# Two heads per load for values as well as keys, in one ring of three 64-KB slots, in a one-core decode block

## The chip, the cores and the metric

The kernel runs on one core of a Trainium2 chip. The metric is the device time in microseconds of one execution; the time before is the median of three runs. A profile of one further execution gives the span, what each engine did and what the DMA engines moved.

## The reference

One token (x, 640 wide) goes through an attention block over a cache of 16384 positions and 32 heads, and then a gated feed-forward block. Both are conditioned by a vector c (adaptive layer norm).

```python
mod = (silu(c) @ w_mod)                      # 640 -> 6 x 640
sa, ca, ga, sb, cb, gb = mod's six parts
h = layernorm(x) * (1 + ca) + sa
q = (h @ wq) as 32 heads of 128
scores = q . k_cache * 128 ** -0.5           # k_cache: 32 heads x 16384 x 128, bf16
p = softmax(scores)
o = p . v_cache                              # v_cache: 32 heads x 16384 x 128, bf16
x = x + ga * (o as one row of 4096 @ wo)
h = layernorm(x) * (1 + cb) + sb
x = x + gb * ((silu(h @ w_gate) * (h @ w_up)) @ w_down)
```

Keys and values are 134 MB each; every byte is read once and used for one multiplication.

## The kernel before, in words

**The order of work.** The kernel lists operations, each with an engine, a position (a number) and the operations it depends on. Each engine's list is sorted by position, so an engine runs its list in order and a wait holds up whatever is behind it. All large loads are issued from the sync engine's list (L71) into one queue, whose transfers run one after the other. `BU(u)` and `EU(u)` are the planned begin and end of unit u; they only order the lists.

**Keys, on VectorE.** A unit is two heads (15 units; the last two heads are units of one). A load of two heads puts 64 KB in each of 128 partitions: 64 partitions per head, 256 positions in each. In place, VectorE multiplies the keys by the query, which is laid out over the partitions (`qbc`, L577, in two pieces), folds the 128 products of a position to 64, 32 and 16 by adding halves (L600; L595 for the first fold of unit 0), and reduces 16 to one score (`S_sb`, L602). Then comes the maximum per partition (L604). The keys lie in `kbig`, two slots of 64 KB per partition: the keys of unit u+2 are loaded once L602 of unit u is done.

**Softmax.** TensorE turns the maxima to a row (L464), VectorE takes the top of each head (L466), TensorE spreads it (L474), ScalarE takes the exponentials (`P_k`, L492). The scores lie 64 partitions to a head, while the values lie 128 partitions to a head, so four products with `place` (L504) move the exponentials to that layout (`P_sb`, evacuated in L508).

**Values, on TensorE.** The values of one head are one load of 32 KB per partition into `vbig`, two slots of 32 KB. 32 products per head (L529) have four positions of `P_sb` as weights and 512 values as the moving side; ScalarE evacuates (L540), and per four heads L547 picks the right parts and turns them into columns (`OT_ps`). L554 divides by the softmax sum (L515 to L518), and L559 to L565 lay eight heads (four in the last group) out for the product with wo (L670). The last head's values come in three pieces and are multiplied position by position (L631). The last four heads' rows of wo come in a layout of their own.

**Before and after.** w_mod (one load of 37.5 KB per partition) and wq come ahead of the keys; w_mod's space is the second key slot, wq's the value slots. The first keys come in two halves. At the end wo goes into the first key slot, the feed-forward weights into the second (L733 gate and up, L751 down, whose weights come in pieces).

Of the kernel before, what the change touches and what calls it, by code (L numbers as in the profile page):

```python
# [141 lines left out]
def build(nc, A_x, A_k, A_v, A_wq, A_wo, B_wg, B_wu, B_wd, c_in, w_mod, out):  # L142
# [10 lines left out]
    GQ = 4  # L153
    PVB = 5
    NU = H // 2 - 1
    T2 = 2 * TT
    UNITS = [(2 * u, 2) for u in range(NU)] + [(H - 2, 1), (H - 1, 1)]

    GROUPS = [(0, 8), (8, 8), (16, 8), (24, 4)]
    HD = 28  # L160
    assert H % GQ == 0 and all(128 % n == 0 for _, n in GROUPS) and GROUPS[-1][0] + GROUPS[-1][1] == HD < H
# [4 lines left out]
    def BU(u):  # L166
        return 20.0 + PERIOD * UNITS[u][0]

    def EU(u):
        return BU(u) + 18.6 * UNITS[u][1]  # L170

    es = ExitStack()
    with es:
# [11 lines left out]
        KS = T2 * 128  # L185
        kbig = sb("kbig", [128, 2 * KS], BF16)
        vbig = sb("vbig", [128, 2 * TT * 128], BF16)
        vring = vbig[:].rearrange("p (s t d) -> p s t d", s=2, t=TT)
        assert max(WM_E, FFN_E, H * D) <= KS and WQ_E <= 2 * TT * 128
        wm_v = kbig[:, KS:KS + WM_E].rearrange("p (k n) -> p k n", k=KC)  # L190
        wq_v = vbig[:, 0:WQ_E].rearrange("p (k n) -> p k n", k=KC)
        wo_v = kbig[:, 0:H * D].rearrange("p (k n) -> p k n", k=H)
        wg_v = kbig[:, KS:KS + KC * F].rearrange("p (k n) -> p k n", k=KC)
        wu_v = kbig[:, KS + KC * F:KS + 2 * KC * F].rearrange("p (k n) -> p k n", k=KC)
        wd_v = kbig[:, KS + 2 * KC * F:KS + 2 * KC * F + FCH * D].rearrange("p (k n) -> p k n", k=FCH)
        acc_sb = sb("acc_sb", [128, 512], F32)
        sel = sb("sel", [128, 4, 4], F32)
        qbc = sb("qbc", [128, len(UNITS), 128], BF16)
        S_sb = sb("S_sb", [128, T2], F32)
        P_k = sb("P_k", [128, T2], BF16)  # L200
        P_sb = sb("P_sb", [128, 2, TT], BF16)
        ident_f = sb("ident_f", [128, 128], F32)
        place = sb("place", [128, 2, 2, 128], BF16)
        ramp = S_sb[:, 0:128]
        gm2 = sb("gm2", [1, 2], F32)
        ones_f = sb("ones_f", [128, 128], F32)
        ones_bf = sb("ones_bf", [128, 128], BF16)
# [3 lines left out]
        Z = sb("Z", [128, len(GROUPS), 128], BF16)  # L211
        A_sb = sb("A_sb", [128, HD], BF16)
        On = sb("On", [128, H - HD], BF16)
        x_row = sb("x_row", [KC, 128], BF16)
        o_row = sb("o_row", [KC, 128], BF16)
        x_res = sb("x_res", [128, KC], F32)
        c_one = acc_sb[0:1].bitcast(BF16)[:, 0:D]
        x_one = qbc[0:1].rearrange("p u d -> p (u d)")[:, 0:D]
        pm = sb("pm", [128, len(UNITS)], F32)
        nb = sb("nb", [128, len(UNITS)], F32)  # L220
        rs = sb("rs", [128, H], F32)
        lnl = sb("lnl", [128, H], F32)
# [38 lines left out]
        R_ps = f_ps[:, 0:2 * TT]  # L261
# [8 lines left out]
        o_onesf = op(DVE, 0.0, lambda e: e.memset(ones_f[:], 1.0), name="ones_f")  # L270
        o_ones = op(DVE, 0.01, lambda e: e.memset(ones_bf[:], 1.0), name="ones")


# [6 lines left out]
        o_pc = op(PE, 1.5, lambda e: e.matmul(A_ps[:, 0:1], lhsT=ramp[0:1, :], rhs=ones_f[0:1, 0:1], start=True, stop=True),  # L280
# [5 lines left out]
        o_pl = op(DVE, 1.72, lambda e: e.memset(place[:], 0.0), name="place0")  # L286
        for hh in range(2):
            for eo in range(2):
                o_pl = op(DVE, 1.73, lambda e, hh=hh, eo=eo: e.tensor_copy(out=place[:, hh, eo, eo:128:2], in_=ident[:, 64 * hh:64 * hh + 64]),
                          deps=[o_ident, o_pl], name="place%d%d" % (hh, eo))  # L290
        o_rs0 = op(DVE, 1.76, lambda e: e.memset(rs[:], 0.0), name="rs0")


        wm_src = w_mod.rearrange("(p k) n -> p k n", p=128)
        wq_src = A_wq.rearrange("(p k) n -> p k n", p=128)
        d_c = plan.dma(0.06, c_one, c_in, "c", name="dma_c", eng="act")
        d_x = plan.dma(0.07, x_one, A_x[0], "x", name="dma_x", eng="act")
        d_wm = plan.dma(0.0, wm_v, wm_src, "wm", name="dma_wmod")
        d_wq = plan.dma(0.1, wq_v, wq_src, "wq", name="dma_wq")


        op(ACT, 0.05, lambda e: e.preload_act_table_set("natural_log_exp_and_others"), name="tbl")


        def to_columns(pos, one, cols, dep, name):
            def f(e):
                last = None
                for k in range(KC):
                    last = e.matmul(cols[:, k:k + 1], lhsT=one[0:1, k:D:KC], rhs=ones_bf[0:1, 0:1], start=True, stop=True)
                return last  # L310
            return op(PE, pos, f, deps=[dep, o_ones], name=name)
        c_col, x_col = f_ps[:, 0:KC], attn_ps[:, 0:KC]
        o_cc = to_columns(0.15, c_one, c_col, d_c, "c_columns")
        o_xc0 = to_columns(0.16, x_one, x_col, d_x, "x_columns")
        o_ec = op(ACT, 0.2, lambda e: e.activation(out=ec[:], in_=c_col, func=ACTF.Exp, scale=-1.0), deps=[o_cc], name="ec")
        o_dd = op(DVE, 0.3, lambda e: e.tensor_scalar_add(out=dd[:], in0=ec[:], scalar1=1.0), deps=[o_ec], name="dd")
        o_rr = op(DVE, 0.4, lambda e: e.reciprocal(out=rr[:], in_=dd[:]), deps=[o_dd], name="rr")
        o_sc = op(DVE, 0.5, lambda e: e.tensor_tensor(out=silu_c[:], in0=c_col, in1=rr[:], op=ALU.mult), deps=[o_rr], name="silu_c")

        def layernorm_ops(pos, src_f32, src_dep, sum_ap, c0, tag, xc_t):  # L320

            o_tot = op(PE, pos, lambda e: e.matmul(st_ps[:, c0:c0 + 1], lhsT=ones_f[:], rhs=sum_ap, start=True, stop=True),
# [6 lines left out]
            o_tot2 = op(PE, pos + 0.3, lambda e: e.matmul(st_ps[:, c0 + 1:c0 + 2], lhsT=ones_f[:], rhs=st[:, c0 + 1:c0 + 2], start=True, stop=True),  # L329
# [24 lines left out]
        o_mod = op(PE, 2.0, lambda e: f_mod(e, wm_v, 0, 2, lambda o, k: slice(o + k, o + D, KC)), deps=[d_wm, o_sc], name="mod_mm_a")  # L354
# [9 lines left out]
        def q_ops(pos, g, wv, n0, ddep, h0, h1):  # L364
            n = h1 - h0
            b = g % 2
            prev = o_qev.get(g - 2)

            def f_q(e):
                last = None  # L370
                for k in range(KC):
                    last = e.matmul(q_ps[b][:, 0:n * 128], lhsT=h_col[:, k:k + 1].broadcast_to([128, 128]),  # L372
                                    rhs=wv[:, k, n0:n0 + n * 128], start=(k == 0), stop=(k == KC - 1))
                return last
            o_q[g] = op(PE, pos, f_q, deps=[ddep, o_h, prev], name="q_mm%d" % g)
            u0 = h0 // 2
            parts = [(slice(64 * hh, 64 * hh + 64), u0, 2, hh) for hh in range(2)]
            if u0 + 2 > NU:
                parts = [(s_, u0, 1, hh) for s_, u0, _, hh in parts]
            for s_, u, m, hh in parts:  # L380
                o_qev[g] = op(ACT, pos + 0.1, lambda e, s_=s_, u=u, m=m, hh=hh: e.activation(  # L381
                    out=qbc[s_, u:u + m], in_=q_ps[b][s_, 0:n * 128].rearrange("p (u h d) -> p u h d", h=2, d=128)[:, 0:m, hh, :], func=ACTF.Copy),
                    deps=[o_q[g]], name="qbc%d_%d" % (g, hh))
            if u0 + 2 > NU:
                o_qev[g] = op(ACT, pos + 0.1, lambda e: e.activation(
                    out=qbc[:, NU:NU + 2], in_=q_ps[b][:, (n - 2) * 128:n * 128].rearrange("p (h d) -> p h d", d=128), func=ACTF.Copy),
                    deps=[o_q[g]], name="qbc_rows")
            for u in range(u0, NU + 2 if u0 + 2 > NU else u0 + 2):
                o_qbc[u] = o_qev[g]

        o_qbc = [None] * len(UNITS)
# [5 lines left out]
        o_mod_b = op(PE, 2.65, lambda e: f_mod(e, wm_v, 2, 6, lambda o, k: slice(o + 128 * k, o + 128 * (k + 1))), deps=[d_wm, o_h], name="mod_mm_b")  # L397
        o_modc = op(ACT, 2.66, lambda e: e.activation(out=modb[:], in_=mod_ps[:, 2 * KC:6 * KC], func=ACTF.Copy), deps=[o_mod_b], name="mod_b")
# [5 lines left out]
        kv = lambda t, h: t[0, h].rearrange("(p t) d -> p t d", p=128)  # L404
        d_k = [None] * len(UNITS)
        d_v = [None] * H
        o_red = [None] * len(UNITS)
        o_free = [None] * len(UNITS)
        o_pv = [None] * H
        o_acc = [None] * H  # L410
        o_diag = {}
        o_rl = {}
        o_z = [None] * H
        o_on = [None] * H
        TL = BU(NU + 1)
        VSPLIT = [0, TT // 2, 3 * TT // 4, TT]

        def kslot(u):
            if u < NU:
# [93 lines left out]
        def sums(q, pos, h0, n):  # L513
# [6 lines left out]
            for i in range(h0, h0 + n):  # L520
                o_rl[i] = r
# [101 lines left out]
        for h in range(HD, H - 2):  # L623
            o_on[h] = o_on[H - 2]
# [188 lines left out]
```

## Time and profile before

| what | us |
|---|---|
| median of three runs (684.04 to 684.44) | 684.13 |
| the profiled execution | 684.22 |
| its span | 682.4 |
| VectorE busy | 612.9 (90%) |
| TensorE busy, products | 329.8 (48%) |
| ScalarE busy | 66.2 (10%) |

The core read 290.48 MB. The span is the time from the first to the last thing that the profile records; the execution's time is 1.8 us longer. In the groups of instructions "out<-in" names the tiles, the shapes are partitions x elements, and the numbers after the bar are total busy time, mean ns of one instruction and the idle time before them. The chain of waits follows the work that ended last from the end to the start. The DMA share is the mean busy share of the core's 16 DMA engines.

### The profile page before, as it was taken

To read this page: it belongs to the slowest core of one execution; us is meant where nothing else is said; L and a number is where in the kernel's file an instruction comes from. 1 tells how busy PE (TensorE), PEld (TensorE's weight loads), DVE (VectorE), ACT (ScalarE), POOL (GpSimd) and SP (SyncE) were. 2 spreads that over 40 slices of the span, in tenths; PEclk is the share of its full clock that TensorE was granted. 3 is DMA by queue.
4 is the path that set the end of the run, shared out by engine and by line. 5 is a ranking of instruction groups with operands and counts; after the bars stand their busy time and mean duration, and the time that the engine had idled before them with its cause. 6 is when DMAs were issued, how large, how long until landed. Compare 5 with 4: busy or idle time off the path is not lost.

```text
span 682.4 us, 5973 instructions
## 1 busy us (share of the span) xinstructions
PE 329.8 (48%) x1944; PEld 137.1 (20%) x1946; DVE 612.9 (90%) x195; ACT 66.2 (10%) x210; POOL 0.2 (0%) x4
## 2 busy tenths in 40 slices
PE   2330280917255371908209561917356370827864
PEld 2210020302112120303003220302022120312354
DVE  3079999999999999999999999999999999999900
ACT  1030100101010101001001201011010101011100
POOL 0000000000000000000000000000000000000000
PEclk9985595866759595867757795867759595877965
DMA  9999999999999999999999999999999999999997
GB/s 387 423 459 405 455 427 421 440 427 434 428 436 425 430 440 424 444 424 451 420 457 411 426 453 411 449 413 455 406 451 430 421 448 423 430 433 413 415 413 278
DMA packets 11238, 290.68 MB, mean 426 GB/s; under 512 B 1046, under 2 KB 1752, under 8 KB 3928
## 3 DMA queue, kind: packets, MB, share of 16 engines
q1 hardware_dynamic: 11220, 290.48, 99.2%
q8 instruction: 10, 0.16, 0.1%
q14 instruction: 4, 0.03, 0.0%
q10 hardware_dynamic: 4, 0.00, 0.0%
HBM read 290.48 MB, written 0.00 MB: 426 GB/s over the span
## 4 chain that ended last, share of the span: by engine, by line
DVE 67%; DMA 23%; PE 6%; SPq 3%; ACT 1%; issue 1%
DVE kbig L577 31%; DVE kbig L600 26%; DMA kbig<-in_A_k_cache_dram 17%; DVE S_sb L602 8%; PE psb L529 5%; DMA x_row<-in_A_x_dram 4%; SPq L71 3%; DMA kbig<-in_B_w_down_dram 2%; DVE kbig L595 1%; DVE pm L604 0%; DVE gm L466 0%; ACT P_k L492 0%; PE psb L504 0%; PE psb L547 0%; PE psb L751 0%
## 5 line engine op out<-in xcount | busy, mean ns | idle before, releaser
L577 DVE TENSOR_TENSOR kbig<-kbig,qbc 128x8192 bf16<-128x8192 bf16 (+2 forms) x34 | 278.0, 8175 | 23.3 <-DMA kbig<-in_A_k_cache_dram 23.3
L529 PE MATMUL psb<-vbig,P_sb 128*4 128x512 bf16 (+1 forms) x992 | 258.6, 418 | 22.1 <-DMA vbig<-in_A_v_cache_dram 15.9
L600 DVE TENSOR_TENSOR kbig<-kbig 128x8192 bf16<-128x8192 bf16 (+3 forms) x50 | 238.3, 4766 | 1.7
L529 PEld LDWEIGHTS psb<-vbig,P_sb 128*4 128x4 bf16 (+1 forms) x992 | 88.0, 89 | 185.5 <-issue 88.1
L464 PE MATMUL psb<-ident_f,pm 128*1 128x128 f32 x34 | 9.5, 380 | 189.7 <-DVE pm L604 189.7
L602 DVE TENSOR_REDUCE S_sb<-kbig 128x256 f32<-128x4096 bf16 (+1 forms) x17 | 70.9, 4169 | 0.6
L540 ACT ACTIVATE acc_sb<-psb 4x512 f32<-4x512 f32 x31 | 18.1, 585 | 267.5 <-PE psb L529 267.5
L464 PEld LDWEIGHTS psb<-ident_f,pm 128*1 128x1 f32 x34 | 1.4, 80 | 195.1 <-DVE pm L604 195.1
L474 PE MATMUL psb<-gm,ones_f 1*64 1x1 f32 (+1 forms) x64 | 6.4, 251 | 55.9 <-DVE gm L466 55.9
L504 PE MATMUL psb<-P_k,place 128*128 128x128 bf16 x60 | 9.1, 308 | 22.9 <-ACT P_k L492 22.9
L478 ACT ACTIVATE nb<-psb 128x1 f32<-128x1 f32 x17 | 2.9, 172 | 171.2 <-PE psb L474 171.0
L474 PEld LDWEIGHTS psb<-gm,ones_f 1*64 1x64 f32 (+1 forms) x64 | 4.9, 199 | 61.7 <-DVE gm L466 61.2
L372 PE MATMUL psb<-vbig,h_col 128*128 128x512 bf16 x38 | 10.8, 449 | 10.6 <-DMA vbig<-in_A_wq_dram 10.4
L492 ACT ACTIVATE P_k<-S_sb,nb 64x256 bf16<-64x256 f32 x30 | 15.2, 505 | 0.9
L559 ACT ACTIVATE Z<-msk,on_f 128x16 bf16<-128x16 f32 (+1 forms) x28 | 6.4, 298 | 71.2 <-DVE on_f L554 71.2
L634 DVE TENSOR_TENSOR On<-psb,rl 128x1 bf16<-128x1 f32 x1 | 0.2, 160 | 13.6 <-PE psb L631 13.6
L547 PE MATMUL psb<-sel,acc_sb 128*128 128x4 f32 (+1 forms) x64 | 8.4, 255 | 4.7 <-ACT acc_sb L540 4.7
L504 PEld LDWEIGHTS psb<-P_k,place 128*128 128x128 bf16 x60 | 5.2, 131 | 24.1 <-ACT P_k L492 24.1
L547 PEld LDWEIGHTS psb<-sel,acc_sb 128*128 128x128 f32 x64 | 7.7, 191 | 8.3 <-ACT acc_sb L540 8.1
L595 DVE TENSOR_TENSOR kbig<-kbig 128x8192 bf16<-128x8192 bf16 x2 | 8.8, 4424 | 0.1
L381 ACT ACTIVATE qbc<-psb 64x256 bf16<-64x256 f32 (+1 forms) x16 | 5.8, 364 | 23.2 <-PE psb L372 23.1
L678 PE MATMUL psb<-ident,x_row 5*128 5x5 bf16 x1 | 0.2, 181 | 15.8 <-DMA x_row<-in_A_x_dram 15.8
(96 smaller groups left out, 101.8 us busy)
## 6 DMA issues: line engine op xcount, KB each, us to landing
vbig<-in_A_v_cache_dram SPq DMA_DIRECT2D x31, 4096.0 KB, 28.7
kbig<-in_A_k_cache_dram SPq DMA_DIRECT2D x4, 4096.0 KB, 33.4
vbig<-in_A_wq_dram SPq DMA_DIRECT2D x1, 5120.0 KB, 25.5
kbig<-in_w_mod_dram SPq DMA_DIRECT2D x1, 4800.0 KB, 13.9
kbig<-in_A_wo_dram SPq DMA_DIRECT2D x1, 3840.0 KB, 21.7
kbig<-in_B_w_gate_dram SPq DMA_DIRECT2D x1, 2160.0 KB, 19.8
kbig<-in_B_w_up_dram SPq DMA_DIRECT2D x1, 2160.0 KB, 24.6
vbig<-in_A_v_cache_dram SPq DMA_DIRECT2D x1, 2048.0 KB, 19.7
```

Source lines behind the costliest of these rows:

```text
L71: return e.dma_start(out_ap, in_ap)
L464: o_T = op(PE, E + 0.1, lambda e: e.matmul(row_ps, lhsT=pm[:, u:u + 1], rhs=ident_f[:], start=True, stop=True), deps=[o_max[u], o_idf, lnl ...
L474: last = e.matmul(top_ps[w * hh:w * hh + w, :], lhsT=ones_f[0:1, 0:w], rhs=gm2[:, hh:hh + 1], start=True, stop=True)
L492: o_exp[h + hh] = op(ACT, pt + 0.2 + 0.01 * hh, lambda e, p_=p_, hh=hh: e.activation(out=P_k[p_], in_=S_sb[p_, :], func=ACTF.Exp, scale=SC ...
L504: last = e.matmul(R_ps[:, TT * hh:TT * (hh + 1)], lhsT=place[:, hh, eo, :], rhs=P_k[:, TT * eo:TT * (eo + 1)], start=(eo == 0), stop=(eo = ...
L529: return e.matmul(acc_ps[s2][0:4, :], lhsT=P_sb[:, s2, bass.ds(t, 4)], rhs=vbig[:, bass.ds(at, 512)], start=start, stop=stop)
L540: o_acc[h] = op(ACT, pos + 0.05, lambda e: e.activation(out=acc_sb[32 * j:32 * j + 4], in_=acc_ps[s2][0:4, :], func=ACTF.Copy), deps=[o_pv ...
L547: last = e.matmul(OT_ps[:, h0:h0 + n], lhsT=acc_sb[:, 128 * i:128 * (i + 1)], rhs=sel[:, i, 0:n], start=(i == 0), stop=(i == 3))
L577: prev.append(op(DVE, B + (13.0 if u == 0 else 4.5) * c, lambda e, ks=ks[:, a:b, :], qb=qb: e.tensor_tensor(out=ks, in0=ks, in1=qb, op=ALU ...
L595: prev[c] = op(DVE, B + 13.0 * c + 8.7, lambda e, ks=ks[:, a:b, :]: e.tensor_tensor(out=ks[:, :, 0:64], in0=ks[:, :, 0:64], in1=ks[:, :, 6 ...
L600: prev = [op(DVE, E - 14.0 + 0.1 * (8 - math.log2(w)), lambda e, ks=ks, w=w: e.tensor_tensor(out=ks[:, :, 0:w], in0=ks[:, :, 0:w], in1=ks[ ...
L602: o_red[u] = op(DVE, E - 4.0, lambda e, ks=ks, w=w, nt=nt: e.tensor_reduce(out=S_sb[:, 0:nt], in_=ks[:, :, 0:w], axis=AX.X, op=ALU.add), d ...
```

## The change

- The space is one tile `big` of three 64-KB slots. Loads are numbered: keys 0, keys 1, then values 0, keys 2, values 1, keys 3 and so on (`NK`, `NV`), values 14 and values 15 at the end; load n lies in slot n % 3 and waits until load n - 3 has been used. So the values of unit u lie where the keys of unit u were, and the keys of unit u+2 where the values of unit u-1 were. w_mod is in slot 2 at first, wq in slot 1; wo follows in slot 2, the feed-forward weights in slot 0.
- All 32 heads are 16 units of two. Values are loaded two heads at a time, 64 KB per partition, 64 partitions to a head, as the keys are. The exponentials go straight into `P2` (position, head), which is zero where a partition belongs to the other head; the `place` products and their evacuation are gone. A product of the values has 8 columns of `P2` (four positions, two heads) as weights; 64 per unit. The result is evacuated into the slot itself, and `turn` (four products per unit) makes columns of it; it stands behind the next row of maxima in TensorE's list.
- The fold to 16 is split: 32 positions are folded in place and reduced, the other 224 are folded into a buffer `F16`, after which the slot counts as free, and reduced from there.
- w_mod comes in two parts of columns, 2 x 640 ahead of wq and the first keys, 4 x 640 behind the first keys; the first keys come in four parts. The product of the second w_mod part moves behind all queries.
- wo is in four equal groups of eight heads (loads of three groups and one). The last unit's values are one load, multiplied position by position with two columns (256 products). The residual x is made from the x already loaded (`x_chunks`), so its second load is gone. The matrix of ones is one column, read with a step of zero.

```diff
-    UNITS = [(2 * u, 2) for u in range(NU)] + [(H - 2, 1), (H - 1, 1)]
-    GROUPS = [(0, 8), (8, 8), (16, 8), (24, 4)]
+    GROUPS = [(8 * i, 8) for i in range(H // 8)]
+    def NK(u):
+        return 2 * u - 1 if u else 0
+    def NV(u):
+        return 2 * u + 2 if u < NU - 1 else 2 * NU - 1
...
+        def slot(n):
+            return big[:, (n % 3) * KS:(n % 3 + 1) * KS]
+        TS = 32
+        F16 = sb("F16", [128, T2 - TS, 16], BF16)
...
-        d_wm = plan.dma(0.0, wm_v, wm_src, "wm", name="dma_wmod")
+        d_wm = [plan.dma(p_, wm_v[:, :, a:b], wm_src[:, :, a:b], ("wm", a), name="dma_wmod%d" % a) for p_, a, b in ((0.0, 0, 2 * D), (0.3, 2 * D, 6 * D))]
...
+        def free_after(n):
+            kind, u = at[n - 3]
+            return (o_kfree if kind == "k" else o_vfree)[u]
...
+        d_k[0] = load("k", 0, 0.2, [], (0, 64, 128, 192, T2))
+        d_k[1] = load("k", 1, 4.3, [o_q[g] for g in o_q])
...
+                    return e.matmul(acc_ps[b][0:8, :], lhsT=P2f[:, bass.ds(t, 8)], rhs=big[:, bass.ds(at, 512)], start=start, stop=stop)
...
+                    last = e.matmul(OT_ps[:, 2 * u:2 * u + 2], lhsT=acc_v[:, 128 * i:128 * (i + 1)], rhs=ident_f[0:8, 2 * i:2 * i + 2],
+                                    start=(i == 0), stop=(i == 3))
+            o_diag[u] = o_vfree[u] = op(PE, pos, f_diag, deps=[o_acc[u], o_idf, o_on[0]], name="turn%d" % u)
...
+            if u:
+                d_v[u - 1] = load("v", u - 1, B - 1.0, [free_after(NV(u - 1))] if u > 1 else [o_mod_b])
+                if u + 1 < NU:
+                    d_k[u + 1] = load("k", u + 1, B - 0.9, [free_after(NK(u + 1))])
+                else:
+                    d_v[u] = load("v", u, B - 0.9, [free_after(NV(u))])
...
+            o_fa = op(DVE, E - 6.2, lambda e, ks=ks: e.tensor_tensor(
+                out=ks[:, 0:TS, 0:16], in0=ks[:, 0:TS, 0:16], in1=ks[:, 0:TS, 16:32], op=ALU.add), deps=prev, name="fold16a_%d" % u)
+            o_ra = op(DVE, E - 6.1, lambda e, ks=ks: e.tensor_reduce(out=S_v[:, 0:TS], in_=ks[:, 0:TS, 0:16], axis=AX.X, op=ALU.add),
+                      deps=[o_fa] + ([o_exp[u - 1]] if u else []), name="reda%d" % u)
+            o_kfree[u] = op(DVE, E - 6.0, lambda e, ks=ks: e.tensor_tensor(
+                out=F16[:], in0=ks[:, TS:, 0:16], in1=ks[:, TS:, 16:32], op=ALU.add),
+                deps=prev + [o_ra, o_ident], name="fold16_%d" % u)
+            o_red[u] = op(DVE, E - 4.0, lambda e: e.tensor_reduce(out=S_v[:, TS:], in_=F16[:], axis=AX.X, op=ALU.add),
+                          deps=[o_kfree[u]], name="red%d" % u)
...
+            if u:
+                value(u - 1, B + 19.0)
+                turn(u - 1, E + 0.15)
```

## The prediction

> **What bounds the kernel now.** I read the page's slices and DMA line first, then a table of windows, because the chain of waits (67% VectorE) and the slices (VectorE 90%) alone would point to VectorE.
>
> ```profile
> DVE  3079999999999999999999999999999999999900
> DMA  9999999999999999999999999999999999999997
> DMA packets 11238, 290.68 MB, mean 426 GB/s; under 512 B 1046, under 2 KB 1752, under 8 KB 3928
> q1 hardware_dynamic: 11220, 290.48, 99.2%
> ```
>
> Two resources look full. The columns below are window, length, PE, PEld, DVE, ACT, POOL, clock, DMA share, GB/s.
>
> ```profile
> 0.00:38.00 38.00, 15.21 (x192) 10.12 (x195) 5.94 (x33) 5.96 (x18) 0.20 (x4) 1.00 0.96 407
> 114.00:190.00 76.00, 36.78 (x160) 14.03 (x158) 75.66 (x18) 7.12 (x22) 0.00 (x0) 0.70 1.00 433
> 265.00:341.00 76.00, 37.62 (x160) 14.18 (x160) 75.66 (x19) 7.12 (x22) 0.00 (x0) 0.72 1.00 431
> 571.00:648.00 77.00, 47.73 (x195) 17.55 (x195) 76.32 (x25) 8.97 (x29) 0.00 (x0) 0.78 1.00 425
> 670.00:682.40 12.40, 5.05 (x144) 4.45 (x142) 1.15 (x6) 0.18 (x1) 0.00 (x0) 0.50 0.59 226
> ```
>
> The DMA share is 1.00 from 38 us to beyond 648 us. VectorE is idle at both ends (38 us, 34 us), the transfers are not. Which of the two sets the pace inside shows in the chain:
>
> ```profile
> 113.70 4.33 DVE kbig L577
> 151.58 4.33 DVE kbig L577
> 454.52 39.05 DMA kbig<-in_A_k_cache_dram
> 531.07 40.07 DMA kbig<-in_A_k_cache_dram
> ```
>
> Early on VectorE runs back to back: 151.58 - 113.70 = 37.88 us for a unit of two heads (37.80 without L554's multiply). Keys land at 493.57 and 571.14, two units apart: 38.78 us a unit. VectorE started behind the transfers, gained almost 1 us a unit, caught up at 454 us and has waited for keys since. So the end is set by 290.5 MB through one queue that never runs dry. Starting VectorE earlier is worth nothing by itself; only less transfer work, a dry queue or a different tail moves the time.
>
> **The transfers.** The trace's packet records give medians by size: 64 KB 2.422 us, 32 KB 1.216, 16 KB 0.615, 10 KB 0.385, 5 KB 0.196, 2.5 KB 0.102, 1.25 KB 0.056, w_mod's 37.5 KB 1.420. One engine of 16 takes 8 packets of a 128-row load.
> - Values of two heads: 16 x 1.216 = 19.46 becomes 8 x 2.422 = 19.38 us. Medians give 0.08 a pair, minima (1.211, 2.418) 0.03, means (1.2185, 2.4234) 0.11. The pitch of 38.78 lies between minima (38.72) and medians (38.83), so I take 0.05; with the last two key loads 16 pairs, -0.8 (-0.5 to -1.8).
> - The last values no longer come in 16-KB and 8-KB pieces: 8 x (0.615 + 2 x 0.312) = 9.91 becomes 9.69, -0.2.
> - w_mod in two column parts: 8 x 1.420 = 11.36 becomes 40 x 0.102 + 40 x 0.196 = 11.92, +0.6.
> - First keys in four parts: 32 x 0.615 = 19.68 against 19.46, +0.2.
> - wo in four equal groups: 24 x 0.385 + 8 x 0.196 + 32 x 0.056 = 12.60 becomes 32 x 0.385 = 12.32, -0.3.
> - 18 fewer DMAs (65 to 47) at one 9-ns completion packet per engine, and no x_row load: -0.2.
>
> Sum: -0.8 - 0.2 + 0.6 + 0.2 - 0.3 - 0.2 = -0.7 us, bounds -0.4 to -1.7.
>
> The Trainium skill's SBUF page ("SBUF — State Buffer", The DMA setup-cost knee) charges every transfer some 2 us and advises the largest single transfer; by it 18 fewer loads would give back 36 us. In this trace the charge is hidden: loads queue behind each other at share 1.00, so I count nothing for it.
>
> **Does the queue stay full?** This is the doubt. Before, keys had two slots and values two of their own. Now values of unit u go into the slot of keys u, and can be asked for only after the last fold of keys u. The rows for that, and for the split fold:
>
> ```profile
> L577 DVE TENSOR_TENSOR kbig<-kbig,qbc 128x24576 bf16<-128x24576 bf16 x14 | 181.1, 12936 | 0.0
> L600 DVE TENSOR_TENSOR kbig<-kbig 128x16384 bf16<-128x16384 bf16 x14 | 121.7, 8693 | 0.5
> L600 DVE TENSOR_TENSOR kbig<-kbig 128x8192 bf16<-128x8192 bf16 x17 | 75.2, 4425 | 0.6
> L602 DVE TENSOR_REDUCE S_sb<-kbig 128x256 f32<-128x4096 bf16 x15 | 66.3, 4420 | 0.5
> L600 DVE TENSOR_TENSOR kbig<-kbig 128x4096 bf16<-128x4096 bf16 x17 | 39.0, 2292 | 0.6
> ```
>
> The 8192 and 4096 rows give a fold 0.16 us + 0.52 ns per element; 4096 and the single heads' 2048 (2.286 us) give a reduction 0.15 + 1.04. The old fold to 16 and reduction (2.29 + 4.42) become 0.43 + 0.69 (512 elements) and 2.03 + 3.89 (3584): +0.33, with two 0.02-us gaps +0.37. A unit costs VectorE 38.2 us, still 0.5 under the pitch of 38.7; so VectorE waits half a microsecond per unit, and the extra 0.37 costs nothing. Without that cover it costs up to 0.37 x 16 = 6 us.
>
> Keys u land at time 0. The last fold ends at 4.33 + 0.19 + 12.88 + 8.70 + 4.43 + 0.43 + 0.69 + 2.03 + gaps = 33.9 us. The first load of all went from issue (0.73 us) to first packet in 1.0 us, the only such time in the trace, so values u move from 34.9; a busy queue might make it 2. The transfer ahead of them (keys u+1) ends at 38.7, on the quickest engine at 36.7, since landings spread over 2.0 us. No gap; 2 to 4 us spare.
>
> Keys u+2 wait for values u-1: these land at 19.4, the product takes 16.6 us (159.13 in the next fence), to 36; the turn (4 products as at L547, 1.05 us) stands on TensorE behind the row of maxima of unit u, so it ends near 39.9. The sync queue is blocked until then, but values u keep the engines busy until 58, and nothing else stands behind that wait. The top maximum on VectorE needs that row at 43.1 and gets it at 38.9. One P2 buffer in place of two: the exponentials of u come at 44, the product of u-1 ended at 36. Dropping the placement products and their evacuation removes 0.61 + 0.39 us of waiting work, off the path.
>
> **Start.** 4.1 + 12.1 + 4.9 us of transfers come before the first key quarter (w_mod part 1, wq, quarter); before it was 11.4 + 12.1 + 9.7, 33.2 in sum, landing at 38.0. So VectorE starts near 21.1 + 4.8 = 26 us. Four quarters at 4.42 + 2.29 and 12 us of the rest end near 65; keys 1 land at 67.6, where they landed at 67.0. 12 us earlier, and worth nothing: VectorE waits there. The second w_mod part is in by 48, needed at 67.
>
> **Tail.** Order now: keys 15, values 14, values 15, wo, FFN weights, with the same bytes behind them.
>
> ```profile
> 159.13 16.59 PE L529 MATMUL psb<-vbig,P_sb 128*4 128x512 bf16 x64 [0.47 <-ACT P_sb L508]
> 657.55 1.87 PE L631 MATMUL psb<-P_sb,vbig 128*128 128x1 bf16 x64 [2.41 <-DMA vbig<-in_A_v_cache_dram]
> 673.00 2.25 PE L733 MATMUL psb<-h_col,kbig 128*128 128x1 bf16 x70 [2.88 <-DMA kbig<-in_B_w_up_dram]
> 679.27 0.78 PE L751 MATMUL psb<-gu_col,kbig 128*128 128x1 bf16 x20 [0.71 <-DMA kbig<-in_B_w_down_dram]
> ```
>
> Keys 15 land near 610, VectorE ends near 648.2 (it ended at 648.2). Row, turn, top and two exponentials: 651.6. Values 15 are in by 649. 256 products at 1.87 / 64 = 0.029 us: 659. Three wo groups 3.3 us, the last Z, its product and group: 664.3 (before 663.9). FFN input 3.3 us later, 667.6; gate ends 2.3 later, at 669.9, and up weights land at 672.4. 2.5 us spare there, so the end still hangs on the last w_down piece, 0.7 us earlier.
>
> **Sum.** The profiled execution took 684.2 us (span 682.4, 1.8 around it), 0.1 over the median of 684.13. 684.2 - 0.7 = 683.5; from the median, 683.4 us.
>
> **Rivals.**
> 1. Faster by over 0.2% (1.4 us, about what a measurement of this kernel can tell from no change). The 64-KB packets save the means' 0.11 instead of 0.05, sum -1.7, time 682.4. For: means contain the real stalls. Against: most of that excess in the 32-KB mean comes from a few packets near 627 us. 0.24.
> 2. Slower: the split fold writes to a new buffer at the reduction's pace, 1.04 ns per element. Place: the 3584-element fold of every unit, 3.89 instead of 2.03 us; VectorE's unit is then 40.1, values are asked for at 35.8 + 1. It decides as soon as the unit exceeds 38.7, each 0.1 us beyond costing 1.5 us over 15 units: (40.1 - 38.7) x 15 = +21, 705 us. Against: L600 has the same 16-bit steps of one at the fast pace, in place. 0.09.
> 3. Slower in the tail: 256 unrolled products with two columns at 0.06 us instead of 0.029. 8 us more, 2.5 spare: +5.5, 689. Against: 64- and 32-product rows agree on 0.03. 0.11.
>
> The Trainium skill's page "VectorE: DVE Perf Modes" (What auto-detection actually checks) picks the doubled rate by 16-bit operands with a step of one, whatever the buffer; that gives rival 2 nothing and leaves 683.4.
>
> **Numbers.** Forecast 683.4 (0.56). Rival 1 is the chance of faster, 0.24; rivals 2 and 3 that of slower, 0.20. The range 682.1 to 687.5 takes in the bounds of the packet costs and most of rival 3; it leaves out rival 2, the far half of rival 3 and a little below.
>
> **What would show it.** Right: DMA share 1.00 in every window from 38 to 660 us; keys two units apart by 77.4 us; VectorE waiting 0.5 us per unit for keys, first multiply near 26 us, a wait of 2 to 3 us before unit 1; last w_down wait as before. Wrong: windows below 0.98 inside (a dry queue), a VectorE that never waits for keys (rival 2), or attn_bf later than 668 (rival 3).

## The result and the profile after

The changed kernel takes 685.37 us (median of 19 runs, 684.39 to 687.13) against 684.29 us (19 runs, 683.99 to 684.47): ratio 1.0018, 95% interval 1.0011 to 1.0025. It is slower by 1.1 us, and its runs spread over 2.7 us where those of the kernel before spread over 0.5. The forecast was 0.7 us the other way. The profiled execution took 684.7 us, its span 682.9.

The slices and the DMA lines of the page after:

```profile
DVE  2597999999999999999999999999999999999901
DMA  8999999999999999999999999999999999999996
DMA packets 9420, 290.68 MB, mean 426 GB/s; under 512 B 764, under 2 KB 958, under 8 KB 4286
q1 hardware_dynamic: 9402, 290.48, 98.9%
```

A packet is what one of the 16 DMA engines moves at a stretch, such as one partition's 64 KB of a load; a load has landed when all 16 engines have delivered their part. There are fewer packets (9420 for 11238), the same bytes, nearly the same share (98.9% for 99.2%). VectorE starts earlier, as forecast (its first multiply at 24.77 us). The same five windows as before:

```profile
0.00:38.00 38.00, 15.05 (x110) 8.40 (x111) 17.17 (x28) 8.63 (x25) 0.20 (x4) 0.95 0.95 398
114.00:190.00 76.00, 36.71 (x156) 15.20 (x156) 74.72 (x22) 4.55 (x17) 0.00 (x0) 0.70 1.01 435
265.00:341.00 76.00, 37.81 (x158) 15.93 (x158) 74.87 (x22) 5.29 (x18) 0.00 (x0) 0.70 1.00 432
571.00:648.00 77.00, 37.63 (x158) 15.74 (x158) 75.02 (x21) 5.29 (x18) 0.00 (x0) 0.69 0.99 427
670.00:682.90 12.90, 7.72 (x214) 7.07 (x214) 1.71 (x9) 0.86 (x5) 0.00 (x0) 0.50 0.54 208
```

Share 1.00 or 1.01 inside, 0.99 once. By this view the queue stays full. The chain of waits gives the pitch of the keys, and the table of waits what VectorE lost from 60 to 650 us:

```profile
262.53 37.98 DMA big<-in_A_k_cache_dram
340.32 37.59 DMA big<-in_A_k_cache_dram
```

```profile
DVE big L540 <- DMA big<-in_A_k_cache_dram: 11.0, 15, 4.3
```

Keys land at 300.51 and 377.91, 77.40 us for two units: 38.70 a unit, the number forecast. VectorE waits 15 times, 11.0 us in all: 4.3 before unit 1, then 0.48 a unit. Its new instructions cost what the fit of the old rows gave:

```profile
L560 DVE TENSOR_TENSOR F<-big 128x3584 bf16<-128x3584 bf16 x16 | 32.4, 2024 | 0.6
L563 DVE TENSOR_REDUCE S_v<-F 128x224 f32<-128x3584 bf16 x16 | 62.2, 3886 | 0.5
L556 DVE TENSOR_TENSOR big<-big 128x512 bf16<-128x512 bf16 x16 | 6.8, 424 | 0.5
L558 DVE TENSOR_REDUCE S_v<-big 128x32 f32<-128x512 bf16 x16 | 11.0, 686 | 0.6
```

2.02 + 3.89 + 0.42 + 0.69 against the 2.03 + 3.89 + 0.43 + 0.69 of the prediction. The last w_down piece lands at 678.5 us by the landing records, 0.7 us earlier than before (679.2). But the span ends 4.4 us behind it, where it was 3.2. TensorE's timeline of the tail shows why:

```profile
652.87 5.07 PE L579 MATMUL psb<-P,big 128*128 128x2 bf16 x185
659.63 2.05 PE L579 MATMUL psb<-P,big 128*128 128x2 bf16 x71 [1.68 <-issue]
661.54 1.66 PE L599 MATMUL psb<-A_sb,big 128*128 128x1 bf16 x57
665.55 1.84 PE L599 MATMUL psb<-A_sb,big 128*128 128x1 bf16 x63 [2.36 <-issue]
672.39 4.43 PE L655 MATMUL psb<-h_col,big 128*128 128x1 bf16 x140 [1.04 <-DVE h_col L639]
677.16 0.32 PE L673 MATMUL psb<-gu_col,big 128*128 128x1 bf16 x6 [0.34 <-DVE gu_col L664]
678.59 1.93 PE L673 MATMUL psb<-gu_col,big 128*128 128x1 bf16 x64 [1.12 <-issue]
```

The column in brackets is the idle time ahead and what ended it. Three times TensorE stops among products that wait for nothing ("issue"): 1.68 us after 185 products of the last values, 2.36 us after 57 products of wo, 1.12 us after 6 products of down. Before the change every pause among these products was ended by a transfer or by an engine's result, none by "issue". The trace's packet records hold an "instruction" packet of 16 KB at 657.2, 663.2 and 676.2 us, 2.4 us ahead of each resumption. That made theory A: the tail's unrolled products (each written out as instructions of its own, without a loop) run faster than their instructions arrive. Rival theory B: the transfers themselves lose time in 64-KB packets or in the ring.

### The profile page after: what moved, and what is told of

Same layout as the page of the kernel before. It is cut to its first block, busy times and chain, and to the rows that moved or that the text cites. A ratio compares the mean times of both kernels' runs of the same rounds, so it can differ in the third digit from the quotient of the medians.

```text
span 682.9 us, 5976 instructions
## 1 busy us (share of the span) xinstructions
PE 318.8 (47%) x2037; PEld 149.0 (22%) x2038; DVE 616.4 (90%) x215; ACT 52.4 (8%) x179; POOL 0.2 (0%) x4
## 2 busy tenths in 40 slices
DMA packets 9420, 290.68 MB, mean 426 GB/s; under 512 B 764, under 2 KB 958, under 8 KB 4286
## 3 DMA queue, kind: packets, MB, share of 16 engines
q1 hardware_dynamic: 9402, 290.48, 98.9%
## 4 chain that ended last, share of the span: by engine, by line
DMA 46%; DVE 41%; PE 7%; issue 6%; ACT 0%; SPq 0%; DVEq 0%
DMA big<-in_A_k_cache_dram 44%; DVE big L540 16%; DVE big L554 15%; DVE S_v L563 5%; DMA big<-in_A_wq_dram 3%; DVE F L560 2%; PE psb L376 2%; PE psb L503 1%; PE psb L579 1%; DVE S_v L558 1%; PE psb L599 1%; PE psb L655 1%; DVE big L556 1%; DVE pm L565 1%; PE psb L443 0%
## 5 line engine op out<-in xcount | busy, mean ns | idle before, releaser
L484 PE MATMUL psb<-big,P 128*8 (+1 forms) x960 | 243.1, 421 | 192.8 <-DMA big<-in_A_v_cache_dram 192.8
L540 DVE TENSOR_TENSOR big<-big,qbc 128x8192 bf16<-128x8192 bf16 (+1 forms) x34 | 278.1, 8179 | 23.3 <-DMA big<-in_A_k_cache_dram 23.3
L554 DVE TENSOR_TENSOR big<-big 128x8192 bf16<-128x8192 bf16 (+1 forms) x31 | 201.2, 6490 | 1.1
L484 PEld LDWEIGHTS psb<-big,P 128*8 (+1 forms) x960 | 89.1, 93 | 340.6 <-DMA big<-in_A_v_cache_dram 121.6
L563 DVE TENSOR_REDUCE S_v<-F 128x224 f32<-128x3584 bf16 x16 | 62.2, 3886 | 0.5
L560 DVE TENSOR_TENSOR F<-big 128x3584 bf16<-128x3584 bf16 x16 | 32.4, 2024 | 0.6
L503 PE MATMUL psb<-ident_f,big 8*128 8x2 f32 x120 | 20.9, 292 | 0.0
L503 PEld LDWEIGHTS psb<-ident_f,big 8*128 8x128 f32 x120 | 19.7, 244 | 4.2 <-issue 4.2
L459 ACT ACTIVATE P<-S_v,nb 64x256 bf16<-64x256 f32 x32 | 18.5, 578 | 0.7
L558 DVE TENSOR_REDUCE S_v<-big 128x32 f32<-128x512 bf16 x16 | 11.0, 686 | 0.6
```

What stands on the lines that cost most here:

```text
L459: o_exp[u] = op(ACT, pos + 0.03 + 0.01 * hh, lambda e, p_=p_, hh=hh: e.activation(out=P2[p_, :, hh], in_=S_v[p_, :], func=ACTF.Exp, scale= ...
L484: return e.matmul(acc_ps[b][0:8, :], lhsT=P2f[:, bass.ds(t, 8)], rhs=big[:, bass.ds(at, 512)], start=start, stop=stop)
L503: last = e.matmul(OT_ps[:, 2 * u:2 * u + 2], lhsT=acc_v[:, 128 * i:128 * (i + 1)], rhs=ident_f[0:8, 2 * i:2 * i + 2], start=(i == 0), stop ...
L540: prev.append(op(DVE, B + (6.0 if u == 0 else 4.5) * c, lambda e, ks=ks[:, a:b, :], qb=qb: e.tensor_tensor(out=ks, in0=ks, in1=qb, op=ALU. ...
L554: prev = [op(DVE, E - 14.0 + 0.1 * (8 - math.log2(w)), lambda e, ks=ks, w=w: e.tensor_tensor(out=ks[:, :, 0:w], in0=ks[:, :, 0:w], in1=ks[ ...
L558: o_ra = op(DVE, E - 6.1, lambda e, ks=ks: e.tensor_reduce(out=S_v[:, 0:TS], in_=ks[:, 0:TS, 0:16], axis=AX.X, op=ALU.add), deps=[o_fa] + ...
```

## The experiments

Ratios are to the kernel before on the same chip (median 684.0 to 684.3). In the cuts of code "..." stands for lines left out.

**Half of the last products.**

```diff
-            for t in range(T2):
+            for t in range(TT):
```

> Leaves out half of the last unit's value products (128 of 256 positions). Theory A (the tail on TensorE): the unrolled products of the tail run faster than their instructions arrive, one stretch of 128 products per 5 to 6 us, and lose 1.7 + 2.4 us before the feed-forward input is ready. With 128 products fewer (3.7 us and one stretch less) the feed-forward input is ready before its weights again, the end hangs on the last w_down piece, and the time falls to 683 to 683.7, about 1 us under before. Theory B (the transfers: 64-KB packets or the three-slot ring lose time on the way): the last landing sets the end, so the time stays near 685.4.

Measured 684.51 us (683.07 to 687.72), ratio 1.0013 (1.0002 to 1.0024).

```profile
654.12 3.55 PE L579 MATMUL psb<-P,big 128*128 128x2 bf16 x128
660.28 3.36 PE L599 MATMUL psb<-A_sb,big 128*128 128x1 bf16 x120 [2.61 <-DMA big<-in_A_wo_dram]
673.92 2.25 PE L655 MATMUL psb<-h_col,big 128*128 128x1 bf16 x70 [2.99 <-DMA big<-in_B_w_up_dram]
679.54 0.78 PE L673 MATMUL psb<-gu_col,big 128*128 128x1 bf16 x20 [0.63 <-DMA big<-in_B_w_down_dram]
```

The tail did what theory A said: no stall, TensorE waits for wo, up and down weights, and the span ends 3.2 us behind the last landing. But that landing came at 679.5, not 678.5, and the spread stayed (4.7 us here). So theory A held for the tail and did not explain all: something in the transfers varies from run to run.

**Moving the cuts.** 64 or 32 one-element products in idle time of TensorE, the tail's work unchanged.

```diff
+        def f_dummy(e):
+            for _ in range(64):            # 32 in the other kernel
+                last = e.matmul(f_ps[0:1, 256:257], lhsT=one_bf[0:1, :], rhs=one_bf[0:1, :], start=True, stop=True)
+        op(PE, BU(8) + 6.0, f_dummy, deps=[o_ones, o_sc], name="dummy")
```

> Adds 64 tiny products (128 instructions) in idle time of TensorE in unit 7; the work of the tail is the same, only the places where its instructions are cut into 16-KB stretches move by 128 instructions. Theory A, with a stretch of 128 products arriving 5.6 us after the one before it was begun: stalls of 1.9 us near product 249 and 1.7 us before the last wo group, none in the gate or down products; the time falls by about 1 us to 684.2. Theory B: unchanged at 685.4.

> As the kernel with 64 tiny products more, but with 32 (64 instructions). Theory A: three stalls before the feed-forward input is ready (near product 153 of the last values, 25 and 153 of wo), 1.9 + 1.9 + 1.3 us; the time rises by 1 to 2 us to 686.5 to 687.5. Theory B: unchanged at 685.4.

Measured 684.70 us (ratio 1.0014, 1.0003 to 1.0025) and 687.56 us (1.0055, 1.0041 to 1.0068). TensorE's tail with 64:

```profile
652.11 6.78 PE L586 MATMUL psb<-P,big 128*128 128x2 bf16 x249
661.11 0.35 PE L586 MATMUL psb<-P,big 128*128 128x2 bf16 x7 [2.22 <-issue]
667.43 1.21 PE L606 MATMUL psb<-A_sb,big 128*128 128x1 bf16 x40 [2.75 <-issue]
672.12 4.44 PE L662 MATMUL psb<-h_col,big 128*128 128x1 bf16 x140 [1.04 <-DVE h_col L646]
```

and with 32:

```profile
652.68 4.22 PE L586 MATMUL psb<-P,big 128*128 128x2 bf16 x153
658.47 2.90 PE L586 MATMUL psb<-P,big 128*128 128x2 bf16 x103 [1.57 <-issue]
664.67 2.69 PE L606 MATMUL psb<-A_sb,big 128*128 128x1 bf16 x95 [2.63 <-issue]
670.59 0.38 PE L606 MATMUL psb<-A_sb,big 128*128 128x1 bf16 x9 [1.93 <-issue]
679.04 1.04 PE L662 MATMUL psb<-h_col,big 128*128 128x1 bf16 x25 [1.07 <-issue]
```

The stalls stand where they were expected, to within two products: behind 249 of the last values and ahead of the last wo group; behind 153, 25 and (95 + 1 + 31 products on) 151 of wo, then in gate. Counted on, 127 or 128 products (256 instructions) lie from one stall to the next, in the changed kernel too (71 + 57), and the resumptions ahead of and in wo are 5.9 to 6.3 us apart, for products that run in 3.6. The same work is 2.9 us slower in one position than in the other. Theory A is shown. The 1 us that 64 were expected to bring is not: by the ratios to before it is 0.3 us, and such a difference is within what separates two series of the changed kernel (below).

**w_mod in one load.**

```diff
-        d_wm = [... for p_, a, b in ((0.0, 0, 2 * D), (0.3, 2 * D, 6 * D))]
+        d_wm = [... for p_, a, b in ((0.0, 0, 6 * D),)]
```

> Undoes the split of w_mod: one load ahead of wq and the first keys. The packets of w_mod cost 0.6 us less, but the first keys land 7.8 us later, so VectorE starts near 34 us and ends unit 0 near 73, 5 us after keys 1 have landed; values 1 are then asked for at 106 to 107, when the queue has run dry at 104 to 106. Both theories: a dry queue of 1 to 3 us near 106, VectorE catching up at 0.5 us per unit. Theory A: the dry queue delays keys 15 and the whole tail, 686 to 688. Theory B the same, so this run only prices that part of the change.

Measured 686.47 us, ratio 1.0037 (1.0024 to 1.0049). In windows:

```profile
38.00:100.00 62.00, 16.31 (x142) 7.30 (x140) 61.66 (x20) 2.10 (x8) 0.00 (x0) 0.59 1.02 439
100.00:108.00 8.00, 3.52 (x17) 1.22 (x14) 7.86 (x5) 0.59 (x1) 0.00 (x0) 0.88 0.71 272
108.00:340.00 232.00, 113.50 (x475) 49.03 (x475) 229.03 (x65) 16.05 (x55) 0.00 (x0) 0.70 1.00 434
```

Share 0.71 over 8 us: the queue runs dry once, as expected (8 x 0.29 = 2.3 us of all engines lost in that window), and not as a whole again. By the ratios the split of w_mod is worth 1.3 us, 0.3 us against the changed kernel's second series below, so its size is not settled. But a later start of VectorE does empty the queue in this ring. That says that the ring is closer to running dry than the prediction took it to be. From here theory C, that the values are asked for too late, was put to the test with the point of asking moved both ways.

**The fold whole, the slot free after the reduction.**

```diff
-            o_kfree[u] = op(DVE, E - 6.0, lambda e, ks=ks: e.tensor_tensor(
-                out=F16[:], in0=ks[:, TS:, 0:16], in1=ks[:, TS:, 16:32], op=ALU.add),
...
+            prev = [op(DVE, E - 6.2, lambda e, ks=ks: e.tensor_tensor(
+                out=ks[:, :, 0:16], in0=ks[:, :, 0:16], in1=ks[:, :, 16:32], op=ALU.add), deps=prev + [o_ident], name="fold16_%d" % u)]
+            o_red[u] = o_kfree[u] = op(DVE, E - 4.0, lambda e, ks=ks: e.tensor_reduce(out=S_v[:], in_=ks[:, :, 0:16], axis=AX.X, op=ALU.add),
...
```

> Undoes the split of the last fold: the whole fold stays in the slot and the slot counts as free only after the reduction, 37.8 us after its keys landed in place of 33.9. Theory C (the ring asks late: a load needs 3.3 to 4 us from its issue until the last of the 16 engines has its first packet, so at 33.9 + 3.5 single engines already run dry before values u come, and what an engine lost is lost for good): values u start near 41.3, a pair of loads takes 38.7 more, so a unit takes (41.3 + 38.7) / 2 = 40.0 instead of 38.7, 14 units: +18 us, near 703. With the prediction's 1 us from issue to first packet: (38.8 + 38.7) / 2, +0.7 us, near 686.

Measured 703.96 us, ratio 1.0288 (1.0274 to 1.0302).

```profile
60.00:340.00 280.00, 122.82 (x534) 50.46 (x535) 264.40 (x62) 17.46 (x60) 0.00 (x0) 0.69 0.99 423
340.00:640.00 300.00, 133.06 (x582) 56.02 (x580) 279.58 (x65) 21.52 (x74) 0.00 (x0) 0.70 0.98 415
```

Theory C gave 703, the prediction's 1 us would have given 686. Asking 3.9 us later costs 18.5 us. By the packet records the engines were without a packet for 12.0 us between 60 and 660 us (mean of 16), and 311 64-KB packets took over 2.45 us, where 2.42 is usual.

**The fold wholly into the buffer.**

```diff
-        F16 = sb("F16", [128, T2 - TS, 16], BF16)
-        S_v = sb("S_v", [128, T2], F32)
+        F16 = sb("F16", [128, T2, 16], BF16)
...
+        S_v = f_ps[:, 0:T2]
...
+                out=F16[:], in0=ks[:, :, 0:16], in1=ks[:, :, 16:32], op=ALU.add), deps=prev + [o_ident], name="fold16_%d" % u)
+            o_red[u] = op(DVE, E - 4.0, lambda e: e.tensor_reduce(out=S_v, in_=F16[:], axis=AX.X, op=ALU.add),
...
```

> The other way: all 256 positions are folded into the buffer (made 8 KB; the scores move to PSUM for the space), so values u are asked for 0.9 us earlier and VectorE's unit is 0.35 us shorter. Theory C: the idle pieces of single engines at the change from keys to values go, keys land 38.70 us apart instead of 38.79, and 0.4 to 1.2 us come back: 684.2 to 685.0, with less spread between runs. With the prediction's 1 us: only the tail starts 0.35 us earlier, 685.0, same spread.

Measured 683.97 us (683.44 to 684.85), ratio 0.9997 (0.9988 to 1.0006); against the changed kernel's ratio of 1.0018 that is 1.4 us back, a little more than expected, and the spread falls to 1.4 us.

```profile
60.00:340.00 280.00, 129.27 (x554) 53.78 (x554) 268.54 (x64) 17.53 (x61) 0.00 (x0) 0.70 1.00 434
340.00:640.00 300.00, 140.16 (x606) 59.07 (x606) 293.38 (x65) 20.34 (x73) 0.00 (x0) 0.70 1.00 433
```

434 and 433 GB/s. By the packet records, between 60 and 660 us no engine is ever without a packet, and 7 of 3873 64-KB packets take over 2.45 us. In the changed kernel the engines were without one for 0.3 us (mean of 16), and 74 packets took longer, 1.1 us (mean of 16) over the usual 2.418. The lost time is so small and so spread over single engines that the share of 1.00 did not show it. Two issues of values in the changed kernel show the delay:

```profile
295.91 0.33 SPq L71 DMA_DIRECT2D big<-in_A_v_cache_dram  x1
373.18 0.33 SPq L71 DMA_DIRECT2D big<-in_A_v_cache_dram  x1
```

By the packet records one engine was without a packet until 299.6 and until 377.2: 3.7 and 4.0 us behind the issue, though the other engines were working. The landing records show what was left to do: at the issue of values the quickest engine had 2.5 to 3.1 us of keys ahead of it in the changed kernel, 3.5 to 3.9 with the full buffer. The packets are the same in both kernels, so theory B's 64-KB packets are out as a cause of their own; what is left of it is the ring, in the form of theory C.

The stalls of TensorE's tail stay with the full buffer:

```profile
651.51 5.07 PE L574 MATMUL psb<-P,big 128*128 128x2 bf16 x185
658.69 2.05 PE L574 MATMUL psb<-P,big 128*128 128x2 bf16 x71 [2.12 <-issue]
664.89 1.84 PE L594 MATMUL psb<-A_sb,big 128*128 128x1 bf16 x63 [2.63 <-issue]
677.91 1.93 PE L668 MATMUL psb<-gu_col,big 128*128 128x1 bf16 x64 [1.10 <-issue]
```

The keys of the last unit land 0.9 us earlier than in the changed kernel (609.9 for 610.9, landing records), and the last products begin 1.4 us earlier (651.51 for 652.87); the stalls are 0.7 us longer together. The last weights land only 0.2 us earlier (678.3 for 678.5). So in this pair of profiles the time lost in the ring reached the end through the keys, VectorE and TensorE's tail, and hardly through the last landing.

**The order in the last unit.**

```diff
-                turn(u - 1, E + 0.15)
+                turn(u - 1, E + (0.15 if u < NU - 1 else 0.215))
...
-        sums(H // GQ - 1, EU(NU - 1) + 0.3)
-        group_out(H - 4, 2, EU(NU - 1) + 0.5, o_diag[NU - 2])
+        sums(H // GQ - 1, EU(NU - 1) + 1.25)
+        group_out(H - 4, 2, EU(NU - 1) + 1.3, o_diag[NU - 2])
```

> Only the order of TensorE's list in the last unit: the turn of unit 14 moves behind the spreading of the tops, the sums behind the last unit's value products. Theory A (the tail's products wait for their instructions): the value products start 1.4 us earlier, every stretch of instructions is asked for as much earlier, the feed-forward input is ready 1.2 to 1.4 us earlier and the time falls by about 1 us to 684.3; the two stalls before it stay. If the last landing alone set the end: unchanged at 685.4.

Measured 684.93 us (684.08 to 688.20), ratio 1.0015 (1.0005 to 1.0025). The gain of 1 us isn't shown: this run can't tell 0.2 us from none, because the transfers' spread covers it. The full buffer took 1.0 us less on the same chip. The profiled execution of the kernel with the other order took 688.2 us, the longest of the nine, and shows what such a run is:

```profile
60.00:340.00 280.00, 125.46 (x548) 52.34 (x548) 270.23 (x78) 18.05 (x61) 0.00 (x0) 0.71 1.00 431
340.00:640.00 300.00, 139.54 (x589) 59.91 (x589) 291.91 (x78) 20.92 (x73) 0.00 (x0) 0.68 1.00 429
```

431 and 429 GB/s; 1.6 us of idle engines and 142 slow packets (over 2.45 us) with 3.8 us in excess, and the last landing at 683.2.

**The changed kernel again, and the bad cuts without a dry engine.**

> The changed kernel once more, unchanged, for a second profile beside the next two. Theories A and C: near 685.4 again with a spread of 1 to 3 us, single engines idle and first packets of 2.5 to 3.5 us in place of 2.42 at some changes from keys to values, and the stalls at the same products (185 of the last values, 57 of wo, 6 of down).

> The kernel with the full 8-KB buffer and 32 tiny products in TensorE's idle time. Theory C is out of play here (no engine runs dry), so theory A is left alone: three stalls before the feed-forward input is ready, near products 153, 25 and 153, and one in gate; 2 us over the kernel with the full buffer, 686 us, with its narrow spread. If the stalls of the first two runs were a by-product of late transfers, it stays at 684.0.

The changed kernel took 686.26 us (685.25 to 688.09), ratio 1.0032 (1.0021 to 1.0043), with 109 slow packets, a last landing at 680.3 and the first two stalls at products 185 and 57 again; the third does not show. The two series of the changed kernel lie 1.0 us apart (1.0018 and 1.0032), so a difference of about 1 us that is read against it from one series to another, as for w_mod and the 64 products, is not settled. The other took 686.23 us (685.66 to 686.77), ratio 1.0031 (1.0019 to 1.0044), with no engine dry and the stalls in their places:

```profile
657.67 2.91 PE L581 MATMUL psb<-P,big 128*128 128x2 bf16 x103 [1.57 <-issue]
663.87 2.69 PE L601 MATMUL psb<-A_sb,big 128*128 128x1 bf16 x95 [2.63 <-issue]
669.78 0.38 PE L601 MATMUL psb<-A_sb,big 128*128 128x1 bf16 x9 [1.93 <-issue]
```

2.3 us over the kernel with the full buffer, whose only difference is 32 tiny products. So the two losses are separate: the cuts cost with every engine busy, and the late asking costs whatever the cuts (with 32 tiny products 1.0055 against 1.0031, 1.6 us). In all four kernels with the full buffer, this one and the two below among them, no engine is without a packet between 60 and 660 us and 7 packets are slow; where values are asked for later, 34 or more are.

**All of it, and wq first.** Full buffer, order in the last unit, 64 tiny products; and then wq ahead of the first w_mod part.

```diff
-        d_wm = [... for p_, a, b in ((0.0, 0, 2 * D), (0.3, 2 * D, 6 * D))]
+        d_wm = [... for p_, a, b in ((0.15, 0, 2 * D), (0.3, 2 * D, 6 * D))]
```

wq stands at position 0.1.

> All of it: full buffer, the other order in the last unit and 64 tiny products in TensorE's idle time. Theories A and C together: stalls near product 249 and before the last wo group, feed-forward input 2.5 us earlier, engines never dry; the end hangs on the last w_down piece again, 3.2 us behind its landing near 677.9: 682.9 to 683.4 us, 0.7 to 1.2 us under before, with a narrow spread.

> The kernel with full buffer, other tail order and 64 tiny products, and wq issued ahead of the first part of w_mod. The first issue is then of 128 packets and not of 640: 0.4 us instead of 0.65 on the sync queue, first packet near 1.75 us as before the change instead of 2.16; queries come 2 to 3 us later, hidden behind the first key quarter. Every transfer 0.4 us earlier: 682.9 us against 683.3.

Measured 683.34 us, ratio 0.9990 (0.9981 to 0.9999), and 683.14 us (682.86 to 683.80), ratio 0.9986 (0.9977 to 0.9995). The second is the fastest kernel of the study, 1 us under before; the two intervals overlap, so the order of the first loads is not shown to matter. TensorE's tail in it:

```profile
660.16 0.30 PE L581 MATMUL psb<-P,big 128*128 128x2 bf16 x6 [2.38 <-issue]
666.36 0.17 PE L522 MATMUL psb<-e,Z 128*128 128x8 bf16 x1 [2.28 <-issue]
678.36 0.78 PE L675 MATMUL psb<-gu_col,big 128*128 128x1 bf16 x20 [0.62 <-DMA big<-in_B_w_down_dram]
```

Two long stalls remain, but the last line waits for the down weights again and the span ends 3.2 us behind their landing (678.3). The first packet went out at 1.75 us as expected, 0.4 us earlier, yet the last landing came only 0.1 us earlier; where the other 0.3 us went is not settled.

## Why the prediction was wrong

**Right.** What bounds the kernel; the sum over the packets (with engines that never run dry the keys of 14 units land 38.73 us apart, 38.78 before); the split fold's cost; VectorE's wait of half a microsecond a unit. The last landing came 0.7 us earlier in the profiled execution, just as forecast, and that is in part luck: time was lost in the ring, and the first packet went out 0.4 us later than before (2.16 for 1.75 us), which the sum leaves out; with the full buffer the last landing came 0.9 us earlier. That an early start of VectorE is worth nothing did not hold in the ring: with w_mod in one load the queue ran dry. Rival 2 (a slow fold into the new buffer) is out: 2.02 us.

**Wrong, first step: "Does the queue stay full?"** The step took 1.0 us from issue to first packet, "a busy queue might make it 2", from one issue into an empty queue, and found 2 to 4 us spare. With its own 2 us the quickest engine had only 36.7 - 35.9 = 0.8 us. Measured, where an engine ran dry its packet came up to 4.0 us behind the issue; at 33.9 that is 37.9, past the 36.7 us at which the quickest engine is done. So single engines run dry for some tenths of a microsecond at some changes from keys to values, and some packets around these changes take up to 3.3 us (4.1 in the second profile) and not 2.42. Both kinds of loss differ from run to run. Moving the point of asking showed the size: 0.9 us earlier gave 1.4 us back (part of it a tail that starts earlier), 3.9 us later cost 18.5 us. The sentence "no gap" was right on the mean of 16 engines and wrong on the single one.

**Wrong, second step: the tail.** It priced 256 products at 0.029 us each from a row of 64 products, 7.5 us, with 2.5 us spare. The pace holds (185 in 5.07 us), but not for 256 products and the 160 behind them in one go: where nothing else holds them up, TensorE stops about every 128 products until the next 16 KB of instructions is there, a term that the sum put at nothing. 1.7 + 2.4 us of stalls stand ahead of the feed-forward input, which came at 672.2 in place of 667.6 (the last products also began 1.3 us later than forecast, 652.9 for 651.6, 0.9 us of it late keys). That used up the 2.5 us spare, so the end hung on TensorE and not on the last landing: +1.2 us. The third stall, 1.1 us, is most of this: with 64 tiny products the gate products began only 0.3 us earlier, the third stall was missing, and the span ended 3.2 us behind the last landing again. In the tail before, the instruction packets of 655.3, 661.5, 672.0 and 677.4 us fall into pauses that a transfer ended, and no stop for instructions shows there. Rival 3 had the place (a tail that becomes the bound) and the wrong mechanism (a slower product). That 685.4 lies within the range is luck: the range reached that far for rival 3's slower product, which did not come.

In the profiled execution the two ends add up: -0.7 at the last landing, +1.2 behind it, +0.5 us in the span. In the second profile the landing was 1.1 us later than before and the rest 4.2 us: +2.1. The medians of the two series moved by +1.1 and +2.2 us.

One citation of the prediction needs a number now. The Trainium skill's SBUF page ("SBUF — State Buffer", The DMA setup-cost knee) puts a roughly fixed 2 us on each transfer, most of it at the transfer's end and a smaller part, some hundred nanoseconds, in its setup. The prediction counted all of it as hidden. What was not hidden here lies ahead of the data and is longer than the page has it: from issue to first packet it was 1.0 us for the first load of all and up to 4.0 us on single engines in the ring. 2.5 to 3.1 us of work left on the quickest engine did not hide it in the changed kernel, 3.3 to 3.9 did in the four kernels with the full buffer.

## What to carry to other kernels

A ring that frees its slot just in time must be checked on the quickest engine and with the time until the last engine has its first packet: here 2.5 to 3.1 us of work left on that engine were too little, 3.3 were enough. A row of 64 unrolled products gives the pace of 64 products; before a tail is made longer, count its instructions in stretches of 256 and look at what was covering the stops. Where a kernel's bound has no slack, an edit that saves nothing on it can still remove the cover of two other things.

## What the runs showed of the hardware

- TensorE's unrolled stream: a stretch of 256 instructions (16 KB) every 5.9 to 6.3 us at the end of the kernel, for 128 products that run in 3.5 to 3.7 us. 64 instructions more or less in an idle place far ahead moved the kernel's time by 2.3 us (32 tiny products with the full buffer against none) and 2.9 us (32 against 64, on one chip). Whether the instructions come faster when the DMA engines are less busy was not tried.
- A load asked for while the engines work left one engine without a packet for up to 4.0 us from its issue; into an almost empty queue (w_mod in one load, at 104.46 us) all 16 had a packet after 2.0 us. Why is open.
- In the changed kernel 74 of 3873 64-KB packets took 2.45 to 3.3 us in place of 2.42, and 54 of these began within 8 us of an issue of values; with the full buffer 7 were slow. That late asking brings them is shown; that they are a start-up which queued packets hide is argued.
